# Two transformer layers on one core: the second layer's last two query chunks taken as four passes of 256 queries, each with its own output projection and feed-forward

## Chip, cores and metric

One Trainium2 chip, one core of it. The metric is the device time of one execution in microseconds (us), lower is better. Times are medians of several executions; each comparison names how many. ScalarE is ACT in the profile, VectorE is DVE, TensorE is PE (its weight loads PEld), GpSimd is POOL, and SyncE is SP, the engine whose queue issues nearly all DMAs of this kernel.

## The reference

Two identical layers, the same weights in both, on 2048 tokens of width 512. All arrays are bf16.

```python
def _A_ref(x, wqkv, wo):                # attention: 32 heads of 16
    qkv = (x @ wqkv).reshape(B, S, 3, H, Dh) ...
    p = _softmax(einsum("bhqd,bhkd->bhqk", q, k) * Dh**-0.5)
    return einsum("bhqk,bhkd->bhqd", p, v) ... @ wo
def _B_ref(x, w1, w2):                  # feed-forward, 512 -> 1792 -> 512
    return _silu(x @ w1) @ w2

x = x + _A_ref(_layernorm(x), A_wqkv, A_wo)
x = x + _B_ref(_layernorm(x), B_w1, B_w2)
x = x + _A_ref(_layernorm(x), A_wqkv, A_wo)
x = x + _B_ref(_layernorm(x), B_w1, B_w2)
```

## The kernel before

The program is one long stream of attention **steps**, with everything else (projections, layer norm, feed-forward) slipped in between as *background*. The queries of a layer come in four chunks of 512 (`qc`). For each chunk there are eight *runs* (four groups `g` of eight heads, two parities `par`), and each run walks over 16 key tiles of 128 keys. A block is one head, one key tile and 512 queries; a step takes the four heads of a run for one key tile. Three of the four blocks go through ScalarE's exp (one alone in `s1`, two together in `s2`), the fourth is made by VectorE and GpSimd from the bits of the float ("d" blocks).

```python
RUNS += [(1, qc, 0, ORDER, range(NKT)) for qc in range(2, NC)]   # layer 2, chunks 2 and 3

def score(blk, out):                       # one block's scores: 32 rows of the array
    L, qc, pi, g, par, kt, j = blk
    r = slice(32 * j, 32 * j + 32)
    nc.tensor.matmul(out, lhsT=KT[L, kt // 4][r, g, ...], rhs=QT[g][r, par, :], start=True, stop=True)

def to_o(key, j, lhsT, rhs, stop=False):   # probabilities times values: 32 columns of the array
    nc.tensor.matmul(o_tiles[key][32 * j : 32 * j + 32, :], lhsT=lhsT, rhs=rhs, ...)
```

When all eight runs of a chunk are done, its output projection and feed-forward become background for the next chunk's steps. Three places in their code:

```python
def load_wo():                             # the projection weight lives in the buffer of hT
    wo[0] = hpool.tile([P, FT, 512], BF16, name="wo", tag="hT")      # hpool has one buffer
    load(wo[0][:, 0:CT, :], A_wo...)

class W1:                                  # first feed-forward weight, 14 tiles of 128 KB
    def __init__(self):
        self.tiles = {}
        for ft in range(2):
            self.load(ft)
    def load(self, ft):
        if ft < FT:
            self.tiles[ft] = w1pool.tile([P, CT, P], BF16, name="w1", tag="w1")   # three buffers
            load(self.tiles[ft][:], B_w1...[:, :, ft * P : (ft + 1) * P])
    def get(self, ft):
        self.load(ft + 2)                  # two tiles ahead
        return self.tiles.pop(ft)

def ffn(L, c):
    ...
    w1 = W1()
    yield part(need=("fT", L, c))
    hT = hpool.tile([P, FT, 512], BF16, name="hT", tag="hT")
    for ft in range(FT):                   # 14 blocks, one weight tile each
        w = w1.get(ft)
        h_ps = yield from mm4("h_ps", ...)
        silu_tanh(h_ps, t_sb[:]) ...
    for tq in range(4): ...                # second product, 14 matmuls for each 128 queries
    if (L, c) != (1, NC - 1):
        load_wo()                          # only now is hT's buffer free again
```

The last chunk has no stream left to hide in, so its projection and feed-forward run alone behind it (`tail`), for all 512 queries.

The softmax here doesn't subtract the row's maximum and nothing guards it: scores larger than these inputs give would overflow.

Of the kernel before, what the change touches and what calls it, by code (L numbers as in the profile page):

```python
# [28 lines left out]
class Background:  # L29
# [10 lines left out]
    def add(self, label, gen, first=False):  # L40
        i = len(self.queue)
        if first:
            i = max([k + 1 for k, item in enumerate(self.queue) if item[2] is not None], default=0)
        self.queue.insert(i, [label, gen, None])
# [183 lines left out]
def kernel(  # L228
# [57 lines left out]
    RUNS += [(1, qc, 0, ORDER, range(NKT)) for qc in range(2, NC)]  # L286
# [156 lines left out]
    def ln_transpose(i, xns, dst, copy=nc.vector.tensor_copy):  # L443

        t_ps = bank("t_ps", BF16).rearrange("p (u c q) -> p u c q", c=CT, u=2)
        for u in range(2):
            for ct in range(CT):
                nc.tensor.transpose(  # L448
                    t_ps[:, u, ct, :], xns[u][:, ct * P : (ct + 1) * P], ident[:, :]
                )  # L450
        copy(out=dst[:, i : i + 2, :, :], in_=t_ps)  # L451

    def ln_chunk(c, dst):

        for i in (0, 2):
            mv, rstd = stats.pop((c, i))
            yield part(need=("rstd", c, i))
            for u in range(2):
                yield part(0.45, need=("xn", xn_count[0] - XN_BUFS))
                xn = ln_apply(c, i + u, mv[:, u, :], rstd[:, u, :])  # L460
                transpose(dst[:, i + u, :, :], xn)
                bg.done["xn", xn_count[0]] = bg.model.landed
                xn_count[0] += 1
# [13 lines left out]
    def ln_ffn(L, c):  # L477
        fTs[L, c] = xslot(L, "fT")
        yield from ln_chunk(c, fTs[L, c])
# [109 lines left out]
    def by_dma(L, qc, pi, g, par):  # L589
        return pi == 0 and (L, qc, g, par) != (1, NC - 1, ORDER[-1], 1)  # L590

    def group_out(L, qc, pi, g, par, oT):
# [3 lines left out]

        if by_dma(L, qc, pi, g, par):
            ot = opool.tile([P, 4, P], BF16, name="ot", tag="ot")
            transpose(ot[:], oT[0])
            bg.done["ot", L, qc, g, par] = bg.model.landed  # L600
            yield part(0.25, need=("ot", L, qc, g, par))
            att = ot[:].rearrange("p t (j s) -> p t j s", j=4)
        else:
            at_once = 4 if len(oT) <= 2 else 2
            yield part(pe=0.06 * at_once * len(oT), sums=True)
            att = bank("att").rearrange("p (t j s) -> p t j s", t=4, j=4)
            for tq in range(4):
# [11 lines left out]
        rec = small.tile([P, 4, 4, 1], FP32, name="rec", tag="rec")  # L619
        nc.vector.reciprocal(rec[:], att[:, :, :, 16:17])  # L620
# [3 lines left out]
        else:  # L624
# [3 lines left out]
            out=attn[L, qc][:, :, P * g : P * (g + 1)].rearrange(  # L628
# [3 lines left out]
            in1=rec[:].to_broadcast([P, 4, 4, DH]),  # L632
            op=ALU.mult,
        )

    def out_T(L, qc, i, copy, home):

        a_ps = bank("a_ps", BF16).rearrange("p (u c q) -> p u c q", u=2, c=CT)
        for u in range(2):
            for ct in range(CT):  # L640
                nc.tensor.transpose(  # L641
                    a_ps[:, u, ct, :],
                    attn[L, qc][:, i + u, ct * P : (ct + 1) * P],
                    ident[:, :],
                )
        copy(out=home[:], in_=a_ps)  # L646
        return home
# [10 lines left out]
    def out_proj(L, qc):  # L658
        if (L, qc) == (0, 0):
            load_wo()  # L660
        aT = wo[0][:, CT : 2 * CT, :].rearrange("p t (c q) -> p t c q", c=CT)
        bg.model.sp = max(bg.model.sp, bg.model.scaled)
        for i in range(4):
            transpose(aT[:, i, :, :], attn[L, qc][:, i, :])
        bg.done["aT", L, qc] = bg.model.landed
        yield part(need=("aT", L, qc))
        for i in range(4):
            yield from out_add(qc, i, aT[:, i, :, :])
            if i % 2:
                bg.add_side(None, ln_pair(qc, i - 1))  # L670
# [5 lines left out]
    def silu_mul(ft, h_ps, t_sb, hT):  # L676
        nc.vector.scalar_tensor_tensor(  # L677
            out=hT[:, ft, :], in0=t_sb, scalar=1.0, in1=h_ps, op0=ALU.add, op1=ALU.mult
        )
# [33 lines left out]
    def ffn(L, c):  # L713
        if (L, c) != (1, NC - 1):
            nxt = (c + 1) % NC
            load_x(nxt, x1[nxt] if (L, c) >= (0, NC - 1) else None)
        w1 = W1()
        yield part(need=("fT", L, c))
        fT = fTs.pop((L, c))
        hT = hpool.tile([P, FT, 512], BF16, name="hT", tag="hT")  # L720
        for ft in range(FT):
            w = w1.get(ft)
            h_ps = yield from mm4(
                "h_ps", lambda ct: w[:, ct, :], lambda ct: fT[:, :, ct, :], out=0
            )
# [3 lines left out]
            silu_mul(ft, h_ps, t_sb[:], hT)  # L729
        for tq in range(4):  # L730
            yield part(pe=0.43)
            y_ps = bank("f_ps")
            for ft in range(FT):
                nc.tensor.matmul(  # L734
                    y_ps,
                    lhsT=hT[:, ft, tq * P : (tq + 1) * P],
# [7 lines left out]
            ffn_out(L, c, tq, y_ps)  # L744
            if L == 0 and tq % 2 == 1:
                bg.add_side(None, ln_pair(c, tq - 1))
        if L == 0:
            bg.add_side(("ln", 1, c), ln_attn(1, c))
        if (L, c) != (1, NC - 1):
            load_wo()  # L750
# [18 lines left out]
    def load_w1_tail():  # L769

        w1 = B_w1.rearrange("(ct p) f -> p ct f", p=P)
        for n in range(4):
# [3 lines left out]
            for ft in range(4 * n, min(4 * n + 4, FT)):  # L776
                if n < 3:
                    w1_tail[ft] = some[:, :, P * (ft % 4) : P * (ft % 4 + 1)]
                else:
                    one = w1pool.tile([P, CT, P], BF16, name="w1", tag="w1")  # L780
                    nc.sync.dma_start(one[:], w1[:, :, P * ft : P * (ft + 1)])
                    w1_tail[ft] = one[:]

    def tail(L, qc):

        aT = wo[0][:, CT : 2 * CT, :].rearrange("p t (c q) -> p t c q", c=CT)
        for i, copy in ((0, nc.vector.tensor_copy), (2, nc.scalar.copy)):
            out_T(L, qc, i, copy, aT[:, i : i + 2, :, :])
# [3 lines left out]
        ln = {}  # L792

        def stats_of(i):
            ln[i] = run(ln_stats(qc, (i, i + 1)))

        def apply(i):
            mv, rstd = ln[i]
            return [ln_apply(qc, i + u, mv[:, u, :], rstd[:, u, :]) for u in range(2)]

        for i in range(2):
            run(out_add(qc, i, aT[:, i, :, :]))
        y_ps = {}
        for i in range(2, 4):
            y_ps[i] = bank("y_ps")
            for ct in range(CT):
                nc.tensor.matmul(
                    y_ps[i], lhsT=aT[:, i, ct, :], rhs=wo[0][:, ct, :], start=(ct == 0), stop=(ct == CT - 1)
                )

        def add(i):
            nc.vector.tensor_tensor(
                out=x_sb[qc][:, i, :], in0=x_sb[qc][:, i, :], in1=y_ps.pop(i), op=ALU.add
            )

        stats_of(0)
        add(2)
        warm(6)
        ln_transpose(0, apply(0), fT, nc.scalar.copy)

        def later(k):
            if k == 1:
                add(3)
            elif k == 3:
                stats_of(2)
            elif k == 6:
                xns.extend(apply(2))
            elif k == 9:
                ln_transpose(2, xns, fT, nc.scalar.copy)

        xns = []
        hT = hpool.tile([P, FT, 512], BF16, name="hT", tag="hT")
        for h in range(2):
            cols = slice(256 * h, 256 * (h + 1))
            f_ps = [bank("f_ps") for _ in range(2)]

            def f_part(u, ft):
                tq = 2 * h + u
                nc.tensor.matmul(  # L839
                    f_ps[u],  # L840
                    lhsT=hT[:, ft, tq * P : (tq + 1) * P],
                    rhs=w2_sb[:, ft, :],
                    start=(ft == 0),
                    stop=(ft == FT - 1),
                )

            for k in range(FT):
                h_ps = bank("h_ps")[:, 0:256]
                for ct in range(CT):
                    nc.tensor.matmul(  # L850
                        h_ps.rearrange("p (t q) -> p t q", q=P),
                        lhsT=w1_tail[k][:, ct, :],
                        rhs=fT[:, 2 * h : 2 * h + 2, ct, :],
                        start=(ct == 0),
                        stop=(ct == CT - 1),
                    )
                t_sb = ts[:, k % 4, :]
                silu_tanh(h_ps, t_sb)
                nc.vector.scalar_tensor_tensor(  # L859
                    out=hT[:, k, cols], in0=t_sb, scalar=1.0, in1=h_ps, op0=ALU.add, op1=ALU.mult  # L860
                )
                if k >= LAG:
                    for u in range(2):
                        f_part(u, k - LAG)
                if h == 0:
                    later(k)
            for u in range(2):
                for ft in range(FT - LAG, FT):
                    f_part(u, ft)
                ffn_out(L, qc, 2 * h + u, f_ps[u])  # L870
# [9 lines left out]
    for g in range(NG):  # L880
        mine = [r for r in runs if r[3] == g]
        n = 0
        for a, b in zip([None, *mine], mine):
            if a and a[0:2] != b[0:2]:
                n += 1
                after_a = runs[runs.index(a) + 1]
                q_next.setdefault(after_a[0:5], []).append((*b[0:2], g, n))
            q_of[b[0:5]] = ("q", *b[0:2], g, n)
# [40 lines left out]
    def score(blk, out):  # L929
        L, qc, pi, g, par, kt, j = blk  # L930
        r = slice(32 * j, 32 * j + 32)
        nc.tensor.matmul(  # L932
            out,
# [197 lines left out]
    with tc.manual_schedule(  # L1131
# [156 lines left out]
        with psum_whole("z"):  # L1288
            tail(1, NC - 1)
# [27 lines left out]
```

## Time and profile before

| | before |
|---|---|
| median of 3 runs, before the prediction | 1562.35 us (1560.34 to 1562.45) |
| span of the profiled run | 1555.5 us |
| end of the last exp | 1514.6 us |
| tail behind it | 40.9 us |
| one step of the stream | 1.407 us |

The page's first part gives busy time, share of the span and number of instructions of each engine:

```profile
PE 1467.6 (94%) x13299; PEld 475.1 (31%) x13397; DVE 1033.7 (66%) x1688; ACT 1513.3 (97%) x2193; POOL 1138.7 (73%) x1229
```

Busy time by stretch: columns are the stretch, its length, then for each engine busy us and in brackets the number of instructions, the granted TensorE clock, the share of DMA and GB/s. The first stretch is the first 97 us of layer 2's chunk 2, the second the rest of the stream, the third the tail.

```profile
core 0: us, PE busy (x) PEld busy (x) DVE busy (x) ACT busy (x) POOL busy (x), PEclk, DMA share, GB/s
1139.00:1236.00 97.00, 90.38 (x841) 28.77 (x848) 66.54 (x109) 97.00 (x144) 71.21 (x74) 1.00 0.20 45
1236.00:1514.00 278.00, 268.07 (x2575) 82.66 (x2586) 163.15 (x254) 278.00 (x401) 207.20 (x207) 1.00 0.15 35
1515.00:1555.00 40.00, 34.20 (x238) 20.88 (x233) 22.97 (x52) 13.67 (x31) 1.85 (x4) 1.00 0.04 14
```

ScalarE is busy 97.00 of 97 and 278.00 of 278: it bounds the stream. In the tail it does 13.67 us of work in 40. PE's 93 and 96% in the stream are partly filler, meant to keep its clock up. One step shows this, in the timeline (start, duration, engine, line, operation, output and inputs, count):

```profile
1490.92 0.69 PE L932 MATMUL s_ps<-QT,KT 32*128 32x512 bf16 x3
...
1491.24 0.38 PE L932 MATMUL d_ps<-QT,KT 32*128 32x512 bf16 x1
...
1491.56 0.83 PE L956 MATMUL o_ps<-w_qkv,zero 128*32 128x512 bf16 x12
...
1492.32 0.69 PE L932 MATMUL s_ps<-QT,KT 32*128 32x512 bf16 x3
```

The scores of a step start at 1490.92, the last of them at 1491.24 once the previous small exp has freed the bank, then 12 matmuls on a zero weight fill the step, and the next scores start at 1492.32.

The chain of waits that ended last, in order of time (start, duration, what), shows the tail: last probabilities-times-values, projection, the feed-forward's first half from 1526.71 and second half from 1539.71, and the last addition.

```profile
1514.66 0.82 PE o_ps L956 x10
...
1519.04 1.92 PE y_ps L487 x8
...
1526.71 1.92 PE h_ps L850 x16
...
1539.71 0.45 PE h_ps L850 x4
...
1552.14 0.69 DVE x L682
```

### The profile page before, as it was taken

Reading aid. Unit: us, or ns where it says so; the run is one execution under the profiler, and the core shown is the slowest. Engines: PE = TensorE matmul, PEld = TensorE weight load, DVE = VectorE, ACT = ScalarE, POOL = GpSimd, SP = SyncE. Lnnn points to the kernel's source line nnn. Section 1 sums busy time; section 2 is a strip of 40 time slices with the busy share of each in tenths; the row PEclk is TensorE's granted clock in tenths of the full one; section 3 lists DMA queues with packets and bytes.
Section 4 is the critical chain, followed back from the end, with each engine's and each line's share of the span. In section 5 each row is a group of like instructions: output and inputs, shape, how many; then the busy total and the mean of one; then the engine's idle time right before and its main releaser. Section 6 shows DMA issues by size and latency. Waiting matters only on the chain. (4 is left out here: it accounts for less than half of the span.)

```text
span 1555.5 us, 34303 instructions
## 1 busy us (share of the span) xinstructions
PE 1467.6 (94%) x13299; PEld 475.1 (31%) x13397; DVE 1033.7 (66%) x1688; ACT 1513.3 (97%) x2193; POOL 1138.7 (73%) x1229
## 2 busy tenths in 40 slices
PE   7999999899989999899998999998999899999998
PEld 3222332232322332233332323322332232222325
DVE  6877676667766766666676677676567655676545
ACT  7999999999999999999999999999999999999993
POOL 2888777678877888678886778776777677777760
PEclk9999999999999999999999999999999999999999
DMA  4100022101220112201021010121112110221110
GB/s 142 32 24 2 5 39 61 33 15 45 46 52 22 35 23 51 55 15 46 14 52 41 8 35 9 25 62 29 29 35 65 28 33 14 46 45 25 40 44 15
DMA packets 149443, 55.85 MB, mean 36 GB/s; under 512 B 127776, under 2 KB 148768, under 8 KB 149280
## 3 DMA queue, kind: packets, MB, share of 16 engines
q1 hardware_dynamic: 149280, 53.65, 15.0%
q8 instruction: 105, 1.72, 0.5%
q14 instruction: 58, 0.48, 0.1%
HBM read 28.57 MB, written 4.19 MB: 21 GB/s over the span
## 5 line engine op out<-in xcount | busy, mean ns | idle before, releaser
L1174 ACT ACTIVATE p_sb<-s_ps 128x512 bf16<-128x512 f32 x2026 | 1469.8, 1137 | 2.0 <-PE d_ps L932 1.8
L1083 DVE TENSOR_SCALAR d_y<-d_ps 128x512 uint16<-128x512 f32 x1012 | 698.1, 690 | 444.4 <-PE d_ps L932 400.6
L932 PE MATMUL s_ps<-QT,KT 32*128 32x512 bf16 x3084 | 646.5, 380 | 51.7 <-ACT p_sb L1174 37.8
L932 PE MATMUL d_ps<-QT,KT 32*128 32x512 bf16 x1012 | 389.1, 384 | 2.7 <-DVE d_y L1083 2.1
L932 PEld LDWEIGHTS <-KT 32*128 32x128 bf16 x4096 | 192.6, 91 | 647.9 <-issue 599.5
L956 PE MATMUL o_ps<-p_sb,VA 128*32 128x512 bf16 x3039 | 311.0, 387 | 8.0 <-DVE oB L1063 1.1
L956 PE MATMUL o_ps<-d_y,VA 128*32 128x512 f16 x1012 | 153.3, 380 | 0.0
L956 PEld LDWEIGHTS <-VA 128*32 128x32 bf16 x4096 | 86.5, 95 | 140.9 <-issue 103.2
L734 PE MATMUL f_ps<-w_sb,hT 128*128 128x512 bf16 x350 | 97.1, 382 | 3.9 <-issue 3.2
L956 PEld LDWEIGHTS <-VB 128*32 128x32 f16 x2024 | 78.2, 97 | 55.1 <-issue 0.3
L674 ACT ACTIVATE t_sb<-h_ps 128x512 f32<-128x512 f32 x98 | 90.7, 926 | 1.5 <-PE h_ps L487 1.5
L956 PE MATMUL o_ps<-w_qkv,zero 128*32 128x512 bf16 x1308 | 90.6, 382 | 0.0
L677 DVE SCALAR_TENSOR_TENSOR hT<-t_sb,h_ps 128x512 bf16<-128x512 f32 x98 | 67.2, 686 | 22.2 <-ACT t_sb L674 21.3
L1063 DVE CAST oT<-o_ps 128x512 bf16<-128x512 f32 x64 | 43.6, 681 | 7.7 <-PE o_ps L956 7.7
L410 DVE BATCH_NORM_STATS2 st<-x 128x6 f32<-128x512 bf16 x64 | 43.6, 681 | 1.7 <-DMA x<-in_A_x_dram 1.7
L734 PEld LDWEIGHTS <-hT 128*128 128x128 bf16 x392 | 29.2, 98 | 45.2 <-issue 23.8
L421 DVE TENSOR_SCALAR xn<-x,mv,rstd 128x513 bf16<-128x513 bf16 x64 | 39.8, 634 | 2.8 <-POOL rstd L415 1.3
L487 PE MATMUL k_ps<-xnT,w_qkv 128*128 128x512 bf16 x128 | 35.1, 386 | 1.9 <-DMA xnT<-xn 1.2
L956 PEld LDWEIGHTS <-zero 128*32 128x32 bf16 x1308 | 24.8, 95 | 37.8 <-issue 25.9
L487 PE MATMUL q_ps<-xnT,w_qkv 128*128 128x512 bf16 x136 | 35.6, 382 | 0.0
L414 POOL TENSOR_SCALAR rstd<-mv 128x2 f32<-128x2 f32 x32 | 7.2, 224 | 37.7 <-DVE mv L412 35.8
L487 PE MATMUL v_ps<-w_qkv,xnT 128*128 128x512 bf16 x112 | 33.0, 382 | 1.7 <-issue 0.6
(2301 smaller groups left out, 2103.2 us busy)
## 6 DMA issues: line engine op xcount, KB each, us to landing
wo<-in_A_wo_dram SPq DMA_DIRECT2D x8, 512.0 KB, 3.9
QT<-q SPq DMA_DIRECT2D x240, 16.0 KB, 1.8
x<-in_A_x_dram SPq DMA_DIRECT2D x7, 512.0 KB, 4.2
out_dram<-x SPq DMA_DIRECT2D x16, 128.0 KB, 1.7
w_sb<-in_B_w_dram SPq DMA_DIRECT2D x1, 1792.0 KB, 13.5
w_qkv<-in_A_wqkv_dram SPq DMA_DIRECT2D x3, 512.0 KB, 6.8
w_tail<-in_B_w_dram SPq DMA_DIRECT2D x3, 512.0 KB, 5.1
ot<-oT SPq DMA_TRANSPOSE x45, 2.4
```

What stands on the lines that cost most here:

```text
L410: nc.vector.bn_stats(st[:], x_sb[c][:, i, :])
L414: nc.gpsimd.tensor_scalar_add(rstd[:], mv[:, :, 1:2], float(EPS))
L421: nc.vector.tensor_scalar(out=wide[:].rearrange("p (a b) -> p a b", b=19), in0=x_wide[c][:, D * i : D * (i + 1) + 1], scalar1=mv[:, 0:1], ...
L487: nc.tensor.matmul(ps.rearrange("p (t q) -> p t q", q=P) if len(r.shape) == 3 else ps, lhsT=lhs(ct), rhs=r, start=(ct == 0), stop=(ct == C ...
L674: nc.scalar.activation(t_sb, h_ps, ACT.Tanh, scale=0.5)
L677: nc.vector.scalar_tensor_tensor(out=hT[:, ft, :], in0=t_sb, scalar=1.0, in1=h_ps, op0=ALU.add, op1=ALU.mult)
L734: nc.tensor.matmul(y_ps, lhsT=hT[:, ft, tq * P : (tq + 1) * P], rhs=w2_sb[:, ft, :], start=(ft == 0), stop=(ft == FT - 1),)
L932: nc.tensor.matmul(out, lhsT=KT[L, kt // 4][r, g, (kt % 4) * P : (kt % 4 + 1) * P], rhs=QT[g][r, par, :], start=True, stop=True,)
L956: nc.tensor.matmul(o_tiles[key][32 * j : 32 * j + 32, :], lhsT=lhsT, rhs=rhs, start=(o_count[key][j] == 0), stop=stop,)
L1063: nc.vector.tensor_copy(out=o, in_=o_tiles[key][:])
L1083: nc.vector.tensor_scalar(out=pr["y"][:, len(pr["ds"]), :], in0=s_ps[:], scalar1=float(1024 * SCALE * math.log2(math.e)), scalar2=float(10 ...
L1174: nc.scalar.activation(p_sb, s_ps, ACT.Exp, bias=-SHIFT * math.log(2.0) + math.log(EXP_SUM), scale=float(SCALE),)
```

## The change

The intent: let only 256 queries remain for the tail. Chunks 2 and 3 of the second layer become four passes of 256 queries. A block then is two key tiles for 256 queries instead of one for 512, so exps keep their number and size; every matmul of scores and of values becomes two of 256 columns. Each pass has its own projection and feed-forward, in which two weight tiles share one block of 512 columns.

```diff
-    RUNS += [(1, qc, 0, ORDER, range(NKT)) for qc in range(2, NC)]
+    LAST = 2 * NC - 3
+    PAIRED = (*range(0, 4), *range(8, 12))
+    RUNS += [(1, u, 0, ORDER, PAIRED) for u in range(2, LAST + 1)]
+    def halved(L, u):
+        return L == 1 and u >= 2
+    def tiles_of(L, u):
+        return (u // 2 + 1, range(2 * (u % 2), 2 * (u % 2) + 2)) if halved(L, u) else (u, range(4))
 ... (run ends, layer norm, projection: 4 tiles become tiles_of(L, u); aT gets a buffer of its own)
+    def h_pair(w1, ft, fT, i):
+        for k in range(2):
+            yield part(pe=0.43, held=k > 0)
+            if k == 0:
+                ps = bank("h_ps")
+            w = w1.get(ft + k)
+            for ct in range(CT):
+                nc.tensor.matmul(
+                    ps[:, 256 * k : 256 * (k + 1)]..., lhsT=w[:, ct, :], rhs=fT[:, i : i + 2, ct, :], ...)
+        yield part(0, held=True)
+        return ps
-    def ffn(L, c):
+    def ffn(L, u):
+        n = 2 if halved(L, u) else 1
+        for ft in range(0, FT, n):
+            if n == 1: h_ps = yield from h_whole(w1, ft, fT)
+            else:      h_ps = yield from h_pair(w1, ft, fT, tiles[0])
 ...
-        if (L, c) != (1, NC - 1):
-            load_wo()
+        load_wo()
 ... (tail: one half instead of two)
-    def score(blk, out):
+    def score(blks, outs):
+        for n, kts in enumerate(key_tiles(*blks[0][0:2], blks[0][5])):    # (kt, kt + 4) if halved
+            for (_, _, _, g, par, _, j), out in zip(blks, outs):
+                nc.tensor.matmul(out[:, P * len(q) * n : P * len(q) * (n + 1)], ...)
 ... (to_o likewise, both key tiles added into the same 256 columns)
```

## The prediction

> **What bounds the kernel now.** ScalarE. The table of engines gives ACT 1513.3 us of a 1555.5 us span (97%); by 50-us windows ACT is 50.0 of 50 almost everywhere between 100 and 1500 us. Each step is one exp of 128x512 and one of 128x1024; in the timeline near 1490 us steps repeat every 1.407 us. The loop of the single-buffered score bank just closes in that time: the small exp ends at 1491.187, its next scores run 1491.238 to 1491.609, the next small exp starts at 1491.646 and takes 0.948. Both bind. PE shows 94%, but much is filler (397 zero matmuls, 27.8 us, between 1200 and 1500 us). After the stream comes a serial tail: the chain of waits has the last probabilities-times-values at 1514.66, first hidden matmul 1526.71, first half of the feed-forward to 1539.7, second half to 1551.1, last store and end at 1555.5: 40.8 us with ScalarE mostly idle.
>
> **What the change does.** Only the last 360 us (second layer, chunks 2 and 3) and the tail change.
> - Removed: the tail works on 256 queries instead of 512. One half of the feed-forward (1539.7 to 1551.1 plus its output, about 12.4 us by the chain) goes; the front (transposes of two tiles, smaller copies: 0.70 and 1.02 us become about 0.45) loses about 1.3 us. The tail falls from 40.8 to about 27 us: -14.
> - Added on ScalarE in the stream: one more 256-query feed-forward, 7 tanh of 128x512; each takes 0.93 us but holds back the next start by only 0.485: +3.4. The exps stay equal in number and size.
> - Moved: scores and values become twice as many matmuls of 256 columns. Array time is unchanged: in the tail, 256-column matmuls with new weights follow each other by 0.109 us, 512-column ones by 0.216. Only the score bank now gets its second half 0.109 us later and ends about 0.01 us later (0.109+0.272 against 0.371): up to +2.6 us over 256 steps. The score and exact-power blocks no longer overlap fully (+0.11 us of PE a step); PE's slack before the gated score is about 0.32 us a step, so this is mostly absorbed, but fillers are still planned by the old cost: I allow +2.
> - Twice as many run ends, each with half-size casts, transposes and scalings: off the critical path (DVE 66%, POOL 73%).
>
> Net -14+3.4+2.6+2 = -6; I say **1556 us**, 8 in 10 between **1547 and 1578**. Faster by over 2%: 0.01; within 2%: 0.88; slower by over 2%: 0.11.
>
> **What would show it.** Chain: last values to end about 27 us, not 40.8. ScalarE's windows stay 50 of 50 from 1150 to about 1520. Spacing of the small exps in the last two chunks 1.407 to 1.42.
>
> **What would make it wrong.** The rate of matmul issue. The stream issues 16 load-and-matmul pairs a step, 88 ns each; afterwards 32, 44 ns each. The trace shows a tighter rate only in bursts (transposes 0.056 us; the densest 100 pairs took 8.06 us). The Trainium skill ("TensorE: Matmul & The Clock Gate", Back-to-back issue gap) gives a sustained 81 ns a pair at 128 columns; if such a limit holds for row and column tiles too, PE becomes the bound and the last 360 us grow by a large part. Likewise if weights of a row group cannot be loaded while that same group still multiplies (nothing before shows it): +0.1 us or more a step, 26 us or more.

## More of the kernel before

At the end of a run its sums are cast to bf16 (`oT`) and turned by a transposing DMA (`ot<-oT`), which is put into SyncE's queue at once and waits there for the cast.

The planner that decides when a background part fits models the engines and some transfers. It assumes that a weight tile is there when its matmul comes. The matmuls themselves run in program order.

## The result, and the profile after

| | before | after |
|---|---|---|
| median of 6 runs each | 1562.4 us (1560.34 to 1565.73) | 1579.36 us (1578.47 to 1584.58) |
| ratio | | 1.0112 (95% interval 1.0094 to 1.013) |
| span of the profiled run | 1555.5 us | 1578.7 us |

A ratio here is the mean time of one kernel's runs over the mean of the other's in the same rounds, so it is not quite the ratio of the medians. The result is clearly slower, by about 17 us, where a gain of 6 was predicted, and it lies just above the stated range.

The same three stretches after, cut at the same steps of the stream:

```profile
1141.00:1238.00 97.00, 90.11 (x1540) 43.25 (x1538) 67.32 (x116) 97.00 (x144) 71.84 (x77) 1.00 0.21 45
1238.00:1549.00 311.00, 276.50 (x4608) 136.66 (x4629) 173.41 (x295) 283.28 (x407) 209.72 (x220) 0.93 0.22 50
1550.00:1578.00 28.00, 21.34 (x146) 12.51 (x148) 12.79 (x30) 6.54 (x16) 1.33 (x3) 0.94 0.03 11
```

In the first 97 us, ScalarE is still busy 97.00, although PE now runs 1540 matmuls there instead of 841. In the second stretch the same stream needs 311 us instead of 278, and ScalarE works only 283.28 of them: nearly 28 us idle. The clock has fallen to 0.93. The third stretch, the tail, is 12 us shorter, as intended. In windows of 50 us:

```profile
1150.00:1200.00 50.00, 47.90 (x885) 23.78 (x888) 35.25 (x62) 50.00 (x73) 39.96 (x45) 1.00 0.28 57
1200.00:1250.00 50.00, 45.05 (x699) 20.57 (x700) 31.85 (x52) 50.00 (x76) 34.05 (x36) 1.00 0.14 31
1250.00:1300.00 50.00, 45.52 (x698) 20.59 (x706) 29.38 (x51) 45.46 (x65) 35.11 (x38) 0.93 0.13 33
1300.00:1350.00 50.00, 40.81 (x701) 21.59 (x695) 27.53 (x45) 43.04 (x64) 30.91 (x34) 0.93 0.32 65
1350.00:1400.00 50.00, 44.26 (x720) 21.16 (x722) 28.86 (x50) 44.31 (x63) 34.77 (x38) 0.90 0.19 46
1400.00:1450.00 50.00, 42.88 (x689) 21.06 (x691) 27.18 (x46) 44.55 (x66) 31.54 (x34) 0.93 0.20 49
1450.00:1500.00 50.00, 46.17 (x871) 24.12 (x873) 28.52 (x51) 46.72 (x68) 35.84 (x38) 0.93 0.35 75
1500.00:1550.00 50.00, 45.36 (x768) 22.90 (x772) 25.21 (x42) 48.07 (x70) 32.41 (x33) 0.97 0.16 39
```

ScalarE's idle time starts after 1250 us. The first 256-query pass began at 1141 us, so the halved matmuls alone ran for 110 us without harm. What begins after 1250 us is the first 256-query *projection*, and from 1314 us the first 256-query *feed-forward*. What PE waited for between 1240 and 1552 us (who waited, for what, us in total, times, longest):

```profile
PE y_ps L486 <- DMA wo<-in_A_wo_dram: 6.0, 2, 3.1
PE h_ps L716 <- DMA w_23318<-in_B_w_dram: 5.1, 1, 5.1
...
PE h_ps L716 <- DMA w_25071<-in_B_w_dram: 3.2, 1, 3.2
PE h_ps L716 <- DMA w_27182<-in_B_w_dram: 2.8, 1, 2.8
...
PE h_ps L716 <- DMA w_23626<-in_B_w_dram: 1.7, 1, 1.7
PE h_ps L716 <- DMA w_25379<-in_B_w_dram: 1.7, 1, 1.7
PE h_ps L716 <- DMA w_27490<-in_B_w_dram: 1.6, 1, 1.6
PE h_ps L716 <- DMA fT<-xn: 1.2, 1, 1.2
```

Before, no wait of this kind is found in the corresponding stretch (1236 to 1514 us). The longest entry there is the stream's own:

```profile
PE s_ps L932 <- ACT p_sb L1174: 5.7, 14, 0.4
```

One of the stalls of after, from PE's side and from SyncE's (both in timelines; the bracket is idle time before and who ended it):

```profile
1314.08 0.61 PE L716 MATMUL h_ps<-fT,w_22849 128*128 128x256 bf16 x4
1314.53 0.60 PE L716 MATMUL h_ps<-fT,w_22851 128*128 128x256 bf16 x4
...
1317.05 0.27 PE L928 MATMUL s_ps<-QT,KT 32*128 32x256 bf16 x1 [0.41 <-ACT p_sb L1186]
...
1322.51 1.04 PE L716 MATMUL h_ps<-fT,w_23318 128*128 128x256 bf16 x4 [5.06 <-DMA w_23318<-in_B_w_dram]
1323.34 1.06 PE L716 MATMUL h_ps<-fT,w_23324 128*128 128x256 bf16 x4
```

```profile
1313.06 5.45 SPq L533 DMA_DIRECT2D QT<-q  x8
1318.63 1.19 SPq L329 DMA_TRANSPOSE ot<-oT  x1
1319.86 0.58 SPq L334 DMA_DIRECT2D w_23318<-in_B_w_dram  x1
1320.55 0.44 SPq L334 DMA_DIRECT2D w_23324<-in_B_w_dram  x1
```

PE used the first pair of weight tiles at 1314.08 and asked for the next tile (`w_23318`) at that point of the program. In SyncE's queue that load stands behind eight query loads (5.45 us) and behind a transpose `ot<-oT`, so it is issued at 1319.86 and lands 2.6 us later. PE, in order, stands in front of it for 5.06 us with all scores behind it. The first four matmuls afterwards take 1.04 us for what took 0.61: a clock record at half speed begins at 1320.55.

The other five late tiles of this weight show the same order in SyncE's queue: each of the six was the next entry after a run's transpose `ot<-oT`. In these five SyncE itself stood still first, for 3.4 to 5.8 us, until the cast that the transpose reads was done. For `w_25071`:

```profile
1396.36 0.37 SPq L334 DMA_DIRECT2D w_24998<-in_B_w_dram  x1
1400.70 1.18 SPq L329 DMA_TRANSPOSE ot<-oT  x1
1401.98 1.75 SPq L334 DMA_DIRECT2D w_25071<-in_B_w_dram  x1
```

From 1396.73 to 1400.70 SyncE issued nothing; VectorE's cast of `oT` ended at 1400.64. The load behind it landed at 1405.66, after PE had stood for 3.2 us.

The Trainium skill ("TensorE: Matmul & The Clock Gate", Part 1) says that an idle window of about 3.4 us halves the clock. The trace agrees on the length of the window: its clock records at half speed last 3.413 or 6.827 us each; there are 11 whole ones after and one before (plus a cut one at the end of each). It does not agree that the whole window has to be idle: in the 3.41 us before each of the eight records between 1240 and 1549 us, PE was idle for only 1.2 to 3.2 us by the profile, and the record at 1395.65 follows a single stall of 1.24 us. (No threshold comes out of this: the window from 1334.2 had 1.25 us idle and was followed by full speed.) So even a short stall can be followed by slow matmuls, and a late load can cost more than its wait.

The tail, in the chain of waits after:

```profile
1549.92 0.83 PE o_ps L964 x22
...
1553.49 1.92 PE y_ps L486 x8
...
1561.66 1.65 PE h_ps L845 x8
...
1574.86 0.69 DVE x L673
```

There is one half of the feed-forward left, from 1561.66.

Adding up the profiled runs from the first step of layer 2's chunk 2, with starts of the large exps read one by one from the trace (before, 1.407 us for a step and 0.485 us for a tanh account for every stretch of 32 steps to within 0.1 us):

| | before | after | difference |
|---|---|---|---|
| start of that step | 1139.4 | 1141.0 | +1.6 |
| from there to the end of the last exp | 375.2 | 408.9 | +33.7 |
| of it: 257 steps of 1.407 | 361.6 | 361.6 | 0 |
| of it: 28 or 35 tanh in the background (14 of them chunk 1's), 0.485 each | 13.6 | 17.0 | +3.4 |
| of it: more than steps and tanh account for | 0.0 | 30.3 | +30.3 |
| tail | 40.9 | 28.8 | -12.1 |
| span | 1555.5 | 1578.7 | +23.2 |

The first row is noise of the early part: it was 1139.4 to 1147.5 in the twelve profiles that were read so, whatever the kernel. The profiled run of before took 1557.28 us, less than any of its six timed runs, so the traces differ by 23 us and the timed runs by 17.

Of the 30 us, gaps of ScalarE longer than 0.1 us make up 27.6: 17.5 follow a matmul that waited for a tile of the first feed-forward weight (`w_...`), 8.8 one that waited for the projection weight (`wo`), 1.4 one that waited for the transposed input `fT`; each sum includes the smaller gaps right behind it, while the clock was halved.

### The profile page after: what moved, and what is told of

It reads as the page before. It is cut to its first block, busy times and chain, and to the rows that moved or that the text cites. A ratio compares the mean times of both kernels' runs of the same rounds, so it can differ in the third digit from the quotient of the medians. Undisturbed runs are those within 1.5% of the kernel's fastest.

```text
span 1578.7 us, 39884 instructions
## 1 busy us (share of the span) xinstructions
PE 1465.1 (93%) x15947; PEld 536.1 (34%) x16056; DVE 1034.8 (66%) x1714; ACT 1512.2 (96%) x2185; POOL 1141.8 (72%) x1245
## 5 line engine op out<-in xcount | busy, mean ns | idle before, releaser
L928 PE MATMUL s_ps<-QT,KT 32*128 32x512 bf16 (+1 forms) x3852 | 641.3, 339 | 49.1 <-ACT p_sb L1186 35.3
L928 PEld LDWEIGHTS <-KT 32*128 32x128 bf16 x5120 | 199.9, 91 | 606.0 <-issue 564.9
L928 PE MATMUL d_ps<-QT,KT 32*128 32x512 bf16 (+1 forms) x1268 | 392.5, 342 | 3.1 <-DVE d_y L1095 2.5
L964 PE MATMUL o_ps<-p_sb,VA 128*32 128x512 bf16 (+1 forms) x3807 | 315.2, 346 | 7.0 <-ACT p_sb L1186 1.1
L964 PEld LDWEIGHTS <-VA 128*32 128x32 bf16 x5120 | 121.2, 96 | 138.0 <-issue 105.5
L964 PE MATMUL o_ps<-d_y,VA 128*32 128x512 f16 (+1 forms) x1268 | 154.1, 338 | 0.0
L964 PEld LDWEIGHTS <-VB 128*32 128x32 f16 x2536 | 99.6, 99 | 42.6 <-issue 0.5
L964 PE MATMUL o_ps<-w_qkv,zero 128*32 128x512 bf16 (+1 forms) x1356 | 73.3, 335 | 0.0
L1075 DVE CAST oT<-o_ps 128x512 bf16<-128x512 f32 (+1 forms) x80 | 45.9, 574 | 7.7 <-PE o_ps L964 7.7
L627 POOL TENSOR_TENSOR attn<-ot,rec 128x128 bf16<-128x128 bf16 (+1 forms) x61 | 31.1, 509 | 6.1 <-DVE rec L620 6.0
```

The lines of the kernel that those rows point to most:

```text
L627: scale(out=attn[L, qc][:, 0:n, P * g : P * (g + 1)].rearrange("p t (j s) -> p t j s", s=32)[:, :, :, 16 * par : 16 * par + 16], in0=att[: ...
L928: nc.tensor.matmul(out[:, P * len(q) * n : P * len(q) * (n + 1)], lhsT=KT[L, kts // 4][r, g, (kts % 4) * P : (kts % 4 + 1) * P], rhs=QT[g] ...
L964: nc.tensor.matmul(o_tiles[key][32 * j : 32 * j + 32, 0:w], lhsT=lhsT[k] if real else zero[:], rhs=rhs[:, w * k : w * (k + 1)], start=(n[j ...
L1075: nc.vector.tensor_copy(out=o, in_=o_tiles[key][:, 0 : o.shape[-1]])
```

## Theories

- **A, late weights.** PE runs in order, and the four passes fetch their weights too late. A pass uses two weight tiles in one block where 512 queries used one, but the loads are still asked for two tiles ahead, that is one block; and the projection weight can only be loaded when the feed-forward of the pass before has left its buffer, just when the next pass's projection wants it.
- **B, finer matmuls.** Twice as many matmuls of half the size are more than PE can issue or load weights for, as the prediction feared.
- **C, the clock.** The lower clock is the cause and not the effect.

## Experiments

Ten kernels ran, all with correct results. The runs of before: 1561.11 us median of 11 runs (experiments 1 to 4), 1561.28 (5, 6, 8 and 9), 1560.78 (7 and 10). The change itself was not run again. The median of before moved by up to 1.6 us; the ratios to before do not suffer from that.

### 1. First feed-forward weight resident

```diff
+    class Resident:
+        def get(self, ft):
+            return w1_tail[ft]
-        w1 = W1()
+        w1 = Resident() if halved(L, u) else W1()
-            if t == len(steps) - 3 * NKT:
+            if t == len(steps) - 14 * NKT:
                 load_w1_tail()              # buffers that the tail's copy takes anyway
```

> The changed kernel with the first feed-forward weight loaded whole once, into the places that the tail uses anyway, about 45 us into the first 256-query pass; the 256-query passes no longer fetch it tile by tile. Theory A (the matmul queue, which runs in order, stands still at late loads: of the first feed-forward weight, about 19 us of ScalarE idle in the trace with what follows from it, and of the output projection weight, about 9 us): 17 to 23 us saved of 1579, so about 1557 to 1562, and no wait of h_ps for a weight load left after 1290 us; the wait of y_ps for the projection weight near 1280 us stays. Theory B (twice as many matmuls of half the size are what PE cannot keep up with): within 3 us of 1579. Theory C (the lower TensorE clock is the cause and not the effect): the clock stays near 0.98 and so does the time.

Measured: 1563.53 us, ratio to before 1.0006 (0.9993 to 1.0019). That is 16 us below the change as it was and, within noise, the time of before. No wait of `h_ps` for a weight is left; the two waits of `y_ps` for the projection weight remain, 5.5 us together. A's range was met but for its end (1557 to 1562); B and C expected no gain.

### 2. Projection weight kept

```diff
+    def keep_wo():                          # in a dead V buffer of layer 1
+        wo[1] = vpool.tile([P, 4, VW], BF16, name="wo_kept", tag="VA")[:, :, 0:D]
+        load(wo[1], A_wo...)
 ...
-   ... lambda ct: wo[0][:, ct, :])
+   ... lambda ct: wo[len(wo) - 1][:, ct, :])
-        load_wo()
+        if 1 not in wo:
+            load_wo()
 ...
+            if t == len(steps) - 14 * NKT:
+                keep_wo()
```

> The changed kernel with only the output projection weight kept in a place of its own from the first 256-query pass on, so that it is not fetched again after each feed-forward. Theory A: about 9 us saved, so about 1570, the two waits of y_ps for that load (near 1280 and 1369 us) gone, the waits of h_ps for weight loads unchanged in number (about 6, some 16 us). Theory B: nothing saved.

Measured: 1573.86 us, ratio 1.0071 (1.0054 to 1.0089). That is 5.5 us less than the change, where 9 were expected. The waits for the projection weight are gone, those for the other weight stay: 16.8 us in nine waits (about six were expected).

### 3. Both

The edits of experiments 1 and 2 together; both loads are issued at the same step (the rest of the edit is cut here):

```diff
-            if t == len(steps) - 3 * NKT:
+            if t == len(steps) - 14 * NKT:
...
+            if t == len(steps) - 14 * NKT:
+                keep_wo()
```

> Both weights resident. Theory A: 25 to 30 us saved, about 1549 to 1554, which is 9 to 13 us under the kernel before (tail shorter by 12, 7 more tanh cost 3.4); ScalarE 50 of 50 in every window from 1150 to 1500 us, clock 0.99 or more over the span. Theory B: above 1570, with ScalarE idle in the last 300 us and a clock of 0.98.

Measured: 1554.84 us, ratio 0.9962 (0.9946 to 0.9978). The stalls of the 256-query passes are gone: of the stream's 3.9 us beyond steps and tanh, all but 0.3 lie before 1240 us. A's range (1549 to 1554) was just missed; the trace has a new stall of 3.2 us, in which PE stands until 1201.9, still in the whole-chunk feed-forward of chunk 1: the 2.3 MB of resident loads, asked for at once at 1188 us, delay that feed-forward's own weight tile (issued 1193.74, landed 1200.77) and a run's transpose behind it (landed 1201.07, 5.8 us after its issue instead of 2.4). The second delay ended last: VectorE waited for that transpose, and PE for VectorE.

### 4. Only the halved matmuls, in the kernel before

```diff
+    def halves(L, qc):
+        return (slice(0, 256), slice(256, 512)) if L == 1 and qc >= 2 else (slice(0, 512),)
+    def score(blks, outs):
+        for h in halves(L, qc):
+            for (...), out in zip(blks, outs):
+                nc.tensor.matmul(out[:, h], lhsT=KT..., rhs=QT[g][r, par, h], start=True, stop=True)
 ... (to_o and the fillers in the same way, one key tile, two halves of the queries)
```

> The kernel before with nothing changed but that each score matmul, each probabilities-times-values matmul and each filler of the second layer's chunks 2 and 3 is issued as two of 256 columns. Theory A: same as before, within 3 us, steps stay at 1.407 us. Theory B (issue rate, weights of a row group, more PE time a step): slower by 15 us or more, ScalarE idle spread over these 360 us.

Measured: 1562.27 us, ratio 1.0006 (0.9992 to 1.0019). Steps stay at 1.407 us, and the stretch from chunk 2 to the last exp takes 375.4 us against 375.2. Of the same stretch as above in this kernel:

```profile
1241.00:1519.00 278.00, 269.94 (x4969) 134.24 (x4958) 162.82 (x254) 277.94 (x401) 207.19 (x207) 1.00 0.16 36
```

4969 matmuls instead of 2575 in the same 278 us, and ScalarE is busy 277.94 of them. B is refuted for scores, values and fillers; the halved matmuls of the feed-forward are not in this kernel, but they are in experiment 3, where nothing starves after 1240 us.

### 5. Still streamed, but six tiles ahead

```diff
+    class Ring(W1):                         # eight places in two dead V buffers
+        ... for ft in range(6): self.load(ft)
+        def get(self, ft):
+            self.load(ft + 6)
+            return self.tiles.pop(ft)
-        w1 = W1()
+        w1 = Ring() if halved(L, u) else W1()
```

> The changed kernel still fetching the first feed-forward weight tile by tile in each 256-query pass, 28 more tile loads than before, but six tiles ahead into eight places instead of two ahead into three. If the lead is what lacks: nearly what keeping it resident gave (1563.5), so 1560 to 1566, with no wait of h_ps for a weight load over 0.5 us after 1290 us; the two waits for the output projection weight stay. If the amount of traffic is what costs: within 4 us of 1579.

Measured: 1564.34 us, ratio 1.0022 (0.9996 to 1.0048), the same as with the weight resident within noise. One wait for a tile of 1.1 us is left, more than the 0.5 that was expected. So it is not the 28 more tiles of traffic that cost, it is the lead (with the eight places that it needs; the two were not separated).

### 6. One tile ahead, in the kernel before

```diff
+        def __init__(self, ahead=2): ...
-            self.load(ft + 2)
+            self.load(ft + self.ahead)
-        w1 = W1()
+        w1 = W1(1 if (L, c) == (1, NC - 2) else 2)
```

> The kernel before, in which only the second layer's chunk 2 feed-forward fetches its first weight one tile ahead instead of two. A tile is then asked for one slot (about 2.8 us) before it is used, as a pair of tiles is in the changed kernel; no matmul is halved and nothing else moves. Theory A: slower by 8 to 20 us, with ScalarE idle behind h_ps that waits for a weight load, and clock drops after it. If the stalls needed the halved matmuls: within 3 us of the kernel before.

Measured: 1561.33 us, ratio 1.0002 (0.9985 to 1.0019): no slower, against the expectation. The trace has a single stall in that feed-forward, 2.1 us, with SyncE's queue as follows:

```profile
1377.70 1.19 SPq L320 DMA_TRANSPOSE ot<-oT  x1
1378.94 1.67 SPq L325 DMA_DIRECT2D w<-in_B_w_dram  x3
```

One block of lead just suffices when SyncE is free: from issue to landing it takes 2.2 to 2.7 us, and an undisturbed block comes every 2.9 to 3.3 us. It failed here when the load stood behind a run's transpose. In this feed-forward there are two run ends, one of which made the stall, and no query loads (the last chunk's queries are already there). In the changed kernel run ends come every 11 us instead of 22, two of the three background feed-forwards share the queue with query loads, and the second tile of each pair also waits for a buffer that PE has just left. So a short lead is needed for the stalls, but a short lead alone did not make them here.

### 7. Loads issued from GpSimd's queue

```diff
-        w1 = W1()
+        w1 = W1(nc.gpsimd if halved(L, u) else nc.sync)
 ... (W1.load issues from that queue; for GpSimd the planner is not told of the load)
```

> The changed kernel with its two tiles ahead, three places and the same traffic, but the weight loads of the 256-query passes are issued from GpSimd's queue instead of SyncE's, where they stand behind query loads and behind the transpose of a run's output that waits for that run's last cast. If the queue order is what makes them late: half or more of the 16 us that residence gained is gained, so 1562 to 1571, and the waits of h_ps for a load fall below 1.5 us each. If only the lead is too short: within 4 us of 1579, with six waits as before. A load issued by GpSimd may take longer to issue than one by SyncE, which would show in the trace as time to landing.

Measured: 1584.97 us, ratio 1.0139 (1.0113 to 1.0165). That is no gain on the change; whether it is slower still is not clear, as the intervals overlap (1.0094 to 1.013 for the change). A gain of half or more of the 16 us, as expected if the queue order alone made the loads late, did not come. What PE waited for in the same stretch of this kernel:

```profile
PE h_ps L719 <- DMA w<-in_B_w_dram: 19.4, 22, 2.0
```

The long waits are gone (longest 2.0 us instead of 5.1), but nearly every block now waits a little: 22 times, 19.4 us. A load takes GpSimd 0.75 to 0.97 us to issue, where SyncE's median in the change is 0.45; it stands behind GpSimd's own additions of 1.04 us; and it lands 2.9 us after its issue began (median), instead of 2.5. With one block of lead, this queue was too late as well. The Trainium skill ("DMA: Bandwidth & Descriptors", Specifications, first-byte latency) gives about 1 us for GpSimd's path against 0.6 for SyncE's; the 0.3 us between the landings here (2.86 against 2.52) has that sign.

### 8. Three passes instead of four

Both weights resident (`Resident()` from pass 2 on), chunk 2 whole, chunk 3 in two passes:

```diff
-    LAST = 2 * NC - 3
+    LAST = NC
-    RUNS += [(1, u, 0, ORDER, PAIRED) for u in range(2, LAST + 1)]
+    RUNS += [(1, 2, 0, ORDER, range(NKT))]
+    RUNS += [(1, u, 0, ORDER, PAIRED) for u in range(3, LAST + 1)]
 ...
-        return L == 1 and u >= 2
+        return L == 1 and u >= 3
```

> Both weights resident, chunk 2 taken whole (512 queries) and only chunk 3 in two passes of 256. The tail is as short as with four passes, but the feed-forward of 512 queries, which took about 100 us of the stream before, must end within one 90 us pass. I expect work left over behind the stream: 5 to 25 us slower than four passes with both weights resident (1554.8), so 1560 to 1580. If it ends near 1554 the four passes were not needed.

Measured: 1561.14 us, ratio 0.9998 (0.9978 to 1.0019), 6 us slower than experiment 3. ScalarE hardly starves in the last passes (one gap, of 0.3 us), but 33.6 us lie behind the last exp instead of 28.8. Chunk 2's feed-forward runs from 1384 to 1472 us, most of the last two passes, so that the one of chunk 3's first pass comes late and 16 of its matmuls (3.8 us) fall into the tail. The smaller passes of chunk 2 avoid that.

### 9. Resident loads earlier, used by chunk 1 too

Both weights, as in experiment 3, but:

```diff
-        w1 = W1()
+        w1 = Resident() if (L, u) >= (1, 1) else W1()
-            if t == len(steps) - 3 * NKT:
+            if t == len(steps) - 15 * NKT:
...
+            if t == len(steps) - 15 * NKT:
+                keep_wo()
```

> Both weights resident, loaded about 22 us into the first 256-query pass and used by the feed-forward of chunk 1 too. With both resident loads 45 us in, one stall of 3.2 us was left near 1204 us, where chunk 1's streamed tile queued behind the 2 MB of resident loads. Theory A: that stall goes, 2 to 4 us under 1554.8, about 1551 to 1553; ScalarE never idle over 0.5 us between 1150 us and the end of the stream.

Measured: 1560.68 us, ratio 0.9994 (0.9976 to 1.0012): worse than experiment 3, through a fault of my edit. The rule "take the kept projection weight as soon as it exists" switched the running projection of chunk 1 to a copy still on its way:

```profile
PE y_ps L486 <- DMA wo_kept<-in_A_wo_dram: 6.7, 1, 6.7
```

ScalarE idled 7.3 us for it. It is theory A once more, made by accident.

### 10. The same, with the old copy for chunk 1

```diff
-    def out_add(c, i, aT):
-   ... lambda ct: wo[len(wo) - 1][:, ct, :])
+    def out_add(c, i, aT, kept=False):
+   ... lambda ct: wo[kept][:, ct, :])       # kept = halved(L, qc), in the tail True
```

> As the run before with all passes' first weight resident from 22 us into the first 256-query pass, but the output projection of chunk 1 still reads the copy that was already there. In that run its third tile was switched by my edit to the copy still on its way, and the matmul queue stood still for 6.7 us (7.3 us of ScalarE idle near 1175 us). Theory A: no stall left between 1150 us and the end of the stream; 2 to 5 us under the version with both resident 45 us in (1554.8), about 1550 to 1553.

Measured: 1552.0 us (1549.04 to 1556.08), ratio to before 0.9938 (0.9914 to 0.9961). It beats both kernels: about 9 us below before, 27 below the change. Its three stretches:

```profile
1140.50:1237.50 97.00, 90.85 (x1546) 43.27 (x1538) 67.28 (x116) 97.00 (x144) 71.84 (x77) 1.00 0.21 51
1237.50:1519.00 281.50, 269.66 (x4636) 135.24 (x4629) 174.67 (x295) 281.30 (x407) 209.68 (x220) 1.00 0.11 22
1520.00:1546.00 26.00, 20.09 (x149) 11.70 (x137) 12.79 (x30) 6.53 (x16) 1.33 (x3) 1.00 0.03 11
```

ScalarE is busy 281.30 of 281.50 us, the clock is at 1.00 (C falls: with the loads mended it comes back by itself), and PE issues as many matmuls as in the change. From chunk 2 to the last exp it takes 379.2 us: before's 375.2, plus 3.4 for seven tanh, plus 0.6. The tail takes 27.2.

## Why the prediction was wrong

- *"The tail falls from 40.8 to about 27 us: -14."* Right in kind and nearly in size: 28.8 us in the profiled run of the change, in which a half-clock window fell into the tail, and 27.2 to 27.5 in five variants with the same tail (28.8 and 29.1 in two others, experiments 3 and 7, where such a window fell into it too).
- *"7 tanh of 128x512 ... +3.4."* Right: in experiments 3 and 10, stretches of 32 steps with seven tanh took 48.3 to 48.9 us where those with none took 45.0 to 45.3.
- *"Up to +2.6 us over 256 steps"* and *"fillers ... I allow +2."* Both too large: in the trace of experiment 4 the halved matmuls cost 0.2 us, and its ratio of 1.0006 (0.9992 to 1.0019) is that of no change. PE's slack in a step did absorb them.
- *"Twice as many run ends ... off the critical path."* **This step failed, and with it the list of what is added.** It looked at the busy share of VectorE and GpSimd. The run ends, though, also put twice as many waiting transposes into SyncE's queue (it stood for a run's cast 16 times between 1240 and 1552 us, against 8 times between 1240 and 1514 before), and the list left out that each pass streams the whole first feed-forward weight and reloads the projection weight, at twice the pace for the same lead. The missing term measured 30.3 us in the trace: with -12.1 for the tail and +3.4 for the tanh it makes the change's +21.6 there. By the ratios, residence of both weights took 23 and 27 us off the time (experiments 3 and 10). What was left then is a gain of 6 and of 9 us; that the predicted 6 is among these owes something to luck, since the allowances of 4.6 us for the matmuls were not needed.
- *"What would make it wrong. The rate of matmul issue."* It was wrong for another reason. The densest 200 load-and-matmul pairs of the changed kernel took 8.56 us, 43 ns a pair. The skill's 81 ns a pair does not hold for these row and column tiles. The second worry, weights of a row group that cannot be loaded while the group multiplies, would have shown in experiment 4 too, and did not.
- *"ScalarE's windows stay 50 of 50 from 1150 to about 1520."* This check, named beforehand, failed at the first 50-us window after 1250 us (45.46 of 50) and led straight to the cause.

Shown: late loads of the two weights make the stalls (experiments 1, 2, 3, 5, 10), and neither the number of matmuls (4) nor the traffic (5) does. The traces add that all six late tiles of the first weight stood right behind a run's transpose in SyncE's queue. Open: how the 16 us of the first weight divide between too short a lead and the queue order, since either a longer lead (5) or no load at all (1) removes them. Experiment 6 had the short lead with fewer entries in the queue; it had one stall, behind a transpose, and lost nothing measurable in time; experiment 7 changed the queue but also the cost of issue, and the planner's account of SyncE with it. The cost of the half-clock windows by themselves was not measured separately.

## What to carry to other kernels

When a pass is cut in half, list everything that is fetched per pass, not only the compute: the same prefetch depth in tiles is half the lead in time, and the queue that issues the loads gets more waiting entries ahead of them. On an engine that runs in order, a background matmul that waits for a load stops the foreground too, so look for such waits in the trace before blaming instruction counts; and a weight that several passes use is best brought in once, early, without a burst in front of loads that somebody is about to need. Putting the loads on another queue did not replace the missing lead here (experiment 7).

## What the Trainium skill lacked or had wrong

- "TensorE: Matmul & The Clock Gate", Back-to-back issue gap: it gives 81 ns a matmul, sustained, at 128 columns for streams of weight load and matmul. With four row or column tiles at work and 256 columns each, 200 such pairs ran in 8.56 us, 43 ns a pair; 48 pairs in a burst took 1.47 us. Neither the section nor the page's part on packed tiles gives a rate for a stream of such pairs.
- "TensorEngine Tiling (Array Packing)", Performance Considerations: it gives a fixed overhead for each matmul. Cutting 512 columns into two of 256 in a stream with four tiles cost nothing measurable here, where PE had slack (ratio 1.0006, experiment 4); the page gives no such measurement.
- "Trainium Kernel Development and Optimization", Key Constraints: it says that issuing DMAs from several engines at once only saves the sequencer's issue time. Here it saved none on the whole (ratio 1.0139 against 1.0112 for the change, intervals overlapping). The page does not say what an issue costs on each engine: for a 128 KB load GpSimd took 0.75 to 0.97 us, SyncE 0.45 in the median, and GpSimd had other work in front of it.
- "TensorE: Matmul & The Clock Gate", Part 1: it has the clock halve after one idle window of about 3.4 us. Here half speed also followed windows in which PE was idle for 1.2 to 2.0 of 3.41 us by the profile (six of the eight records between 1240 and 1549 us).
- No page puts a number on what a load loses when it stands in the issuing engine's queue behind a transfer that waits for a semaphore. Here SyncE issued nothing for 4.0 us before a transpose (1396.73 to 1400.70), and the weight tile behind it made PE stand for 3.2 us.
